# Two of nine blocks turn x and q on TensorE instead of VectorE, and block 0 makes its sums of h in two parts

## The chip, the core and the metric

The kernel runs on one core of a Trainium2 chip. The metric is the device time of one execution in microseconds (us); the median of three runs of the kernel before is 1025.14 us. In the profile TensorE is PE, VectorE is DVE, ScalarE is ACT, GpSimd is POOL, and SP is the engine that only issues DMAs. PEld is the loading of weights into TensorE, which overlaps with PE.

## What is computed

An attention without softmax for 8 batches and 8 heads (576 tokens, head size 64), a norm, and a gated feed-forward network, all in float32:

```python
kv = np.einsum('bhsd,bhse->bhde', k, v)
out = np.einsum('bhsd,bhde->bhse', q, kv)
rms = np.sqrt(np.mean(out * out, axis=-1, keepdims=True) + 1e-06)
out = out / rms * g_norm
x = out.transpose(0, 2, 1, 3).reshape(4608, 512)
g = x @ w_gate                       # 512 x 1536
silu = g * (1.0 / (1.0 + np.exp(-g)))
return (silu * (x @ w_val)) @ w_out  # 1536 x 512
```

## The kernel before

The 4608 tokens are cut into nine blocks of 512 (`BLK`); block n takes the last rows of batch n-1 and the first of batch n. Each block has two parts.

**Attention (class `Att`).** `load_kv` and `load_q` bring k, v and q into tiles of the pool `ld` (four buffers). `kv` makes the 64 x 64 products of k and v (L314) into the PSUM pool m (two buffers). `turn` transposes q, so that `product` (L355) can multiply it with kv; `product` also squares the result on ACT and sums it on DVE. `root` takes 1/sqrt by eleven small DVE instructions, `scale` multiplies, and the result has to be transposed again into `x`, with the gain applied on ACT; `sums` makes the sums of parts of x that the feed-forward part needs.

There are two ways to transpose. On PE: a product with the identity into PSUM (`turn_q`, L335, for q; `turn_x`, L402, for x), then a copy by ACT or DVE. On DVE: the stream transpose turns squares of 32 x 32 (L329 for q, L412 for x), and DMAs put these squares in place: on loading, for q (`load_quarters`, 32 small DMAs a block), and for x by `place_x` (L426, 16 DMAs, half on SP's queue, half on ACT's). `TURNED` is the first block whose x goes the second way; `quarters` says the same for q. In the kernel before, block 0 goes the first way and blocks 1 to 8 the second.

**Feed-forward (class `Ffn`).** The products are made by a scheme with seven products in place of eight (Strassen, Winograd's form), as in class `Quad`: products are numbered 1 to 7, and their order is written out by hand. Block 0 makes its up products plainly (`plain_up`, L1018), while the weights arrive and are rounded; `plain_end` then makes the sums of h, and `Down` multiplies h with `w_out` (L551). Block 1 uses the scheme once (`Up`, L551). Blocks 2 to 8 (`DEEP` is 2) use it twice, nested (`Inner`, L714); the summed weights that they need, the leaves, are made by DVE during block 1 (`leaf_steps`) and sent to DRAM (w), and each later block streams them from there through the tiles t (`Stream`, L795: nine buffers, 51 chunks of up to 256 KB a block). The last leaves, those of the weight pairs 4 and 5, stand in the list `latest` and are made during block 1's down stage. Down products 5, 7 and 4 use differences of `w_out` in nine t tiles, made by POOL (`turn_t`); `Stream.enable` opens the stream of the next block.

During the down stage of block n, the attention of block n+1 is laid between the down products: `steps` gives a table from the number of a product to what follows it. Where x goes the second way the whole of the product follows down product 1, `place_x` down product 5, and gain and sums down product 2:

```python
return {1: whole, 5: self.place_x, 2: end}          # n >= TURNED
return {1: lambda: self.half(0, ...), 6: middle, 2: last}   # otherwise
```

Otherwise the product is made in two halves, with `turn_x(0)` and the second half behind down product 6 and `turn_x(1)` behind down product 2; the order of the down products is then 1, 5, 6, 7, 2, 4, 3 in place of 1, 6, 5, 7, 2, 4, 3. In one f32 product of PE the profile counts two pieces, so a down product is 24 pieces of 256 columns.

The order of instructions on an engine is not that of the text alone. A scheduler simulates the engines and issues what is ready, by priority in the order of the text; `tc.issue_after` and `tc.keep_in_program_order` tie an instruction behind another on its engine.

Of the kernel before, what the change touches and what calls it, by code (L numbers as in the profile page):

```python
# [14 lines left out]
P = 128  # L15
# [3 lines left out]
def kernel(  # L19
# [173 lines left out]
    class Att:  # L193


        def __init__(self, n):
            self.n = n

            self.cut, half = divmod(n, 2)
            self.split = half * D  # L200
            self.ps, self.z = {}, None
            self.q, self.k, self.v, self.room = [], {}, {}, None
            self.halves = []
            self.quarters = n > 0

        def parts(self, t):

# [58 lines left out]
                    )  # L266
                    views[j] = t.rearrange("p h (t d) -> p h t d", t=KT)

        def load_quarters(self, i, pairs=(0, 1)):


            if pairs[0] == 0:
                self.q.append(ld_pool.tile([P, LD], F32, name="ld")[:, 0 : 2 * BLK])
            to = self.q[i].rearrange("p (j g d) -> p j g d", j=2, d=P // 4)
            cut = 2 * self.n
            spans = [(self.n - 1, S - D * self.n, 0, cut), (self.n, 0, cut, BLK // 32)]
            for j in pairs:
                for r in range(4):
                    h, d = divmod(r, 2)
                    for b, s0, g0, g1 in spans:  # L280
                        if g1 > g0:
                            nc.sync.dma_start(  # L282
                                out=to[32 * r : 32 * (r + 1), j, g0:g1],
                                in_=q[b, 4 * i + 2 * j + h, s0 : s0 + 32 * (g1 - g0), 32 * d : 32 * (d + 1)].rearrange(
                                    "(g p) d -> p g d", p=32
                                ),
                            )

        def load_q(self, i):
            if self.quarters:  # L290
# [127 lines left out]
        def place_x(self):  # L418
            src = self.turned.rearrange("p i (x c) -> p (i x) c", c=P)
            self.x = x_pool.tile([P, 7, 2, HB], F32, name="x")  # L420
            dst = self.x[:, 0:4].rearrange("p o k (t c) -> p (o k t) c", c=P)
            rows = [slice(32 * r, 32 * (r + 1)) for r in range(4)]
            for a in range(4):
                for b in range(4):
                    queue = nc.scalar if b % 2 else nc.sync
                    placed = queue.dma_start(out=dst[rows[b], :, rows[a]], in_=src[rows[a], :, rows[b]])  # L426
                    if b % 2 == 0:
                        self.placed = placed

        def gain_x(self):  # L430
            for i in range(2):
# [93 lines left out]

    DEEP = 2

    TURNED = 1

    class Quad:  # L530

# [41 lines left out]
    class Up(Quad):  # L573
# [51 lines left out]
        def multiply(self, p):  # L625
            super().multiply(p)
            ffn = self.ffn
            if ffn.n != DEEP - 1:
                return

            if p == 5:
                self.leaf_room = ring().rearrange("p f (s c) -> p (f s) c", c=P)
            if p in (5, 7, 4):
                at = 3 * (5, 7, 4).index(p)
                ffn.making.extend(leaf_steps(self.j, [(self.w[p].unsqueeze(1), (p,))], self.leaf_room[:, at:]))
            if p == 3:
                if ffn.leaf_room is None:
                    ffn.leaf_room = x_pool.tile([P, 3, 7, P], F32, name="xi").rearrange("p a b c -> p (a b) c")
                halves = lambda t: t[self.j].rearrange("p (o i) c -> p o i c", o=2)
                steps = lambda room: leaf_steps(self.j, [(halves(wg), (1, 2)), (halves(wv), (6, 3))], room)  # L640
                if self.j < NP - 2:
                    ffn.later.extend(steps(ffn.leaf_room))
                else:
                    ffn.latest.append(steps)

# [195 lines left out]
    class Down(Quad):  # L841
# [23 lines left out]
        def multiply(self, p):  # L865
            super().multiply(p)
            if p in self.t:
                stream.free((self.ffn.n, p))
            if p == 7:
                stream.enable(self.ffn.n + 1)  # L870
            stream.pump()

# [20 lines left out]
        def after2(self):  # L893
            add(nc.vector, self.o1[:, :, 0:HD], self.ps["a"], self.s)
            if self.final:
                self.ffn.store(self.o1[:, :, 0:HD], 0, slice(0, HD))

            pairs = self.ffn.h.rearrange("p (j e) t -> p e j t", e=2)
            self.s4 = sub(nc.vector, pairs[:, 1, :, 0:HB], pairs[:, 1, :, 0:HB], pairs[:, 0, :, HB:BLK])

        def after7(self):
            o = ring()
# [25 lines left out]
    class Ffn:  # L928
# [52 lines left out]
        def down(self, nxt):  # L981

            down = self.down_
            fill = nxt.steps() if nxt else {}
            for p in (1, 6, 5, 7, 2, 4, 3) if 5 in fill else (1, 5, 6, 7, 2, 4, 3):
                if p == 1:
                    down.turn_t(7, self.ended)
                if p == 6:
                    down.turn_t(4, nxt.halves[0] if nxt and nxt.n >= TURNED else None)

                with tc.issue_after(nxt.multiplied.ins) if self.n == 0 and p in (5, 6) else ExitStack():
                    down.multiply(p)
                self.make(12)
                if p in fill:
                    fill[p]()
                if p in (5, 7) and self.n == DEEP - 1:

                    with tc.issue_after(nxt.scaled.ins), tc.issue_after(nxt.placed.ins):
                        room = self.leaf_room if p == 5 else ring().rearrange("p f (s c) -> p (f s) c", c=P)
                        for step in self.latest.pop(0)(room):  # L1000
                            step()
                if p == 1:

                    with tc.issue_after(nxt.q_turned.ins) if self.n == 0 else ExitStack():
                        down.turn_s3()
# [20 lines left out]
        def plain_end(self):  # L1026

            self.s1 = s_pool.tile([P, NP, HB], F32, name="s1")
            self.h_sums(0, NP, nc.vector)
            self.down_ = Down(self)  # L1030
            self.down_.turn_t(5)

# [33 lines left out]
    for n in range(NB):  # L1066
        ffn = Ffn(n, blocks[n])
        nxt = blocks[n + 1] if n + 1 < NB else None
        if n == 0:

            with tc.issue_after(squared.ins), tc.issue_after(scaled.ins):
                weights(2)
            ffn.plain_up(0, (0,))
            copied = blocks[0].copied
            blocks[0].turn_x(1)
            for f in range(NF):
                with tc.issue_after(blocks[0].copied.ins if f else copied.ins):
                    weights(2 * (f + 2))
                ffn.plain_up(f) if f else ffn.plain_up(0, (1,))
            weights(len(pieces))  # L1080
            pairs = wo.rearrange("p (j e) d -> p e j d", e=2)
            t2(pairs[:, 0, :, HD:DM], pairs[:, 1, :, HD:DM], pairs[:, 0, :, 0:HD])
            nxt.room = x_pool.tile([P, 3, 7, P], F32, name="xi").rearrange("p a b c -> p (a b c)")

            with tc.issue_after(sent.ins):
                for i in range(2):
                    nxt.load_kv(i)
                for i in range(2):
                    nxt.load_q(i)
            ffn.plain_end()  # L1090
            for g in range(2):
                nxt.kv(g)
        else:

            def third():
                nxt.kv(0)
                nxt.load_kv(1)

            def two_thirds():
                nxt.kv(1)  # L1100
                if nxt.n == 2:
                    for i in range(2):
                        nxt.load_q(i)

            fill = {4: third, 8: two_thirds} if nxt else {}
            if n == DEEP:
                for a, at in enumerate((1, 2, 3, 5)):
                    fill[at] = lambda i=a // 2, j=a % 2: nxt.load_quarters(i, (j,))
            ffn.up(fill)
        if nxt:  # L1110
            nxt.turn()
        if 0 < n < NB - 2:
            blocks[n + 2].load_kv(0)
        if DEEP <= n < NB - 2:
            for i in range(2):
                blocks[n + 2].load_q(i)
        ffn.down(nxt)
        if n == 0:
            blocks[2].load_kv(0)

            with tc.issue_after(nxt.halves[0].ins):
                for j in range(NP // 2):
                    t2(wv[j][:, 0:2], wv[j][:, 2:4], wg[j][:, 0:2])
            with tc.issue_after(ffn.down_.s4.ins):
                for j in range(NP // 2, NP):
                    t2(wv[j][:, 0:2], wv[j][:, 2:4], wg[j][:, 0:2])


# [29 lines left out]
```

## Time and profile before

| | |
|---|---|
| three runs, median (lowest, highest) | 1025.14 us (1025.01, 1025.32) |
| the profiled execution | 1025.01 us, span 1023.2 us |
| PE busy, PEld busy | 1006.5 us, 896.9 us |
| DVE, ACT, POOL busy | 701.0 us, 228.0 us, 368.9 us |
| granted TensorE clock | 1.00 |
| first up product of block 0 | 29.7 us |
| block 0, down products | 116.3 to 155.8 us |
| block 1, up; down | 155.8 to 234 us; 234 to 272.9 us |
| DMA | 170.26 MB, mean 166 GB/s |

The profile is of one execution; its times are counted from the span's start. A group of instructions is given by its line in the kernel, engine, operation, and the tiles it writes and reads (`x<-r`). The chain is followed back from the last instruction, at each step to what released it. A busy time of PE comes from modelled ends, so the pace (how far apart starts are) says more than the busy share.

### The profile page before, as it was taken

How to read it: one execution, taken by the hardware profiler on the slowest of the kernel's cores; microseconds unless marked ns; L12 is line 12 of the kernel's file. 1: busy time of each engine (PE TensorE's matmuls, PEld its weight loads, DVE VectorE, ACT ScalarE, POOL GpSimd, SP SyncE). 2: the span in 40 equal slices, each digit the busy share in tenths (PEclk: the TensorE clock that was granted, in tenths of full speed). 3: DMA queues.
4: the chain of work that ended last, by engine and by line, in shares of the span. 5: the costliest groups of instructions: out<-in, count | busy, mean ns of one | idle time of the engine just before them, and what ended most of it. 6: DMA issues, size and time to landing. Idle time of an engine off the chain costs nothing.

```text
span 1023.2 us, 21404 instructions
## 1 busy us (share of the span) xinstructions
PE 1006.5 (98%) x8522; PEld 896.9 (88%) x8522; DVE 701.0 (69%) x1168; ACT 228.0 (22%) x352; POOL 368.9 (36%) x280
## 2 busy tenths in 40 slices
PE   6999999999999999999999999999999999999998
PEld 4544688888999989998999899988998999989997
DVE  2999688998666945685657566665669466946661
ACT  2766111221211212121121211111121211211110
POOL 0000263434045512561246315630555046513670
PEclk9999999999999999999999999999999999999999
DMA  8689633667888367855685568637772766066601
GB/s 224 201 264 275 127 70 113 184 150 167 246 219 245 70 164 204 253 100 119 209 243 146 89 199 246 183 57 200 231 197 50 175 196 188 20 165 205 189 29 42
DMA packets 273844, 170.26 MB, mean 166 GB/s; under 512 B 150608, under 2 KB 241872, under 8 KB 273744
## 3 DMA queue, kind: packets, MB, share of 16 engines
q1 hardware_dynamic: 238800, 164.42, 59.4%
q10 hardware_dynamic: 34880, 4.46, 2.7%
q8 instruction: 68, 1.11, 0.5%
q14 instruction: 32, 0.26, 0.1%
q0 software_dynamic: 64, 0.00, 0.0%
HBM read 138.02 MB, written 22.41 MB: 157 GB/s over the span
## 4 chain that ended last, share of the span: by engine, by line
PE 92%; DVE 3%; DMA 2%; SPq 1%; issue 1%; ACT 1%; DVEq 0%; ACTq 0%
PE b L714 26%; PE b L551 20%; PE c L714 13%; PE c L551 10%; PE a L714 6%; PE a L551 5%; PE b L1018 4%; PE c L1018 4%; PE m L314 2%; PE m L355 1%; DMA h<-in_v_dram 1%; SPq L282 1%; DVE xi L112 1%; DVE r L111 1%; DMA h<-in_k_dram 0%
## 5 line engine op out<-in xcount | busy, mean ns | idle before, releaser
L111 POOL TENSOR_TENSOR r<-r 128x256 f32<-128x256 f32 (+1 forms) x105 | 110.8, 1062 | 301.0 <-DVE r L111 241.1
L111 DVE TENSOR_TENSOR r<-b,r 128x512 f32<-128x512 f32 (+1 forms) x273 | 161.9, 606 | 65.6 <-PE b L714 60.6
L112 POOL TENSOR_TENSOR t<-wo 128x512 f32<-128x512 f32 x81 | 114.5, 1437 | 213.4 <-DVE wo L111 103.5
L111 DVE TENSOR_TENSOR r<-c,r 128x512 f32<-128x512 f32 (+1 forms) x179 | 108.4, 617 | 88.1 <-PE c L714 54.5
L714 PE MATMUL b<-x,t 128*128 128x128 f32 x1092 | 151.2, 275 | 0.0
L111 DVE TENSOR_TENSOR r<-a,r 128x512 f32<-128x512 f32 (+1 forms) x99 | 62.5, 631 | 113.5 <-PE a L551 71.1
L714 PEld LDWEIGHTS b<-x,t 128*128 128x128 f32 x1092 | 136.5, 192 | 0.8
L714 PE MATMUL c<-xi,t 128*128 128x128 f32 x840 | 112.4, 275 | 0.4 <-DVE xi L111 0.4
L113 POOL TENSOR_TENSOR h<-r 128x1024 f32<-128x1024 f32 (+1 forms) x40 | 81.9, 2064 | 78.1 <-DVE r L111 75.4
L714 PEld LDWEIGHTS c<-xi,t 128*128 128x128 f32 x840 | 102.9, 192 | 0.5 <-DVE xi L111 0.5
L551 PE MATMUL b<-wo,h 128*128 128x256 f32 x432 | 100.0, 383 | 0.1
L551 PE MATMUL b<-t,h 128*128 128x256 f32 x432 | 96.9, 381 | 0.0
L551 PEld LDWEIGHTS b<-t,h 128*128 128x128 f32 x432 | 81.5, 190 | 11.4 <-issue 0.2
L551 PEld LDWEIGHTS b<-wo,h 128*128 128x128 f32 x432 | 79.8, 190 | 13.0 <-DVE h L113 2.5
L728 ACT COPY r<-b 128x512 f32<-128x512 f32 x63 | 36.9, 586 | 211.5 <-PE b L714 206.4
L714 PE MATMUL b<-xi,t 128*128 128x128 f32 x588 | 79.7, 276 | 0.0
L714 PEld LDWEIGHTS b<-xi,t 128*128 128x128 f32 x588 | 72.4, 192 | 0.0
L714 PE MATMUL b<-x,wg 128*128 128x128 f32 x336 | 52.7, 279 | 0.2 <-DVE x L112 0.2
L714 PE MATMUL b<-x,wv 128*128 128x128 f32 x336 | 51.3, 275 | 0.0
L551 PE MATMUL a<-wo,h 128*128 128x256 f32 x216 | 48.3, 379 | 0.0
L551 PE MATMUL c<-wo,h 128*128 128x256 f32 x216 | 48.1, 379 | 0.0
L551 PE MATMUL c<-t,s 128*128 128x256 f32 x216 | 48.1, 379 | 0.0
(128 smaller groups left out, 1556.8 us busy)
## 6 DMA issues: line engine op xcount, KB each, us to landing
t<-w SPq DMA_DIRECT2D x336, 256.0 KB, 3.6
out_dram<-r SPq DMA_DIRECT2D x17, 512.0 KB, 3.1
ld<-in_k_dram SPq DMA_DIRECT2D x26, 288.0 KB, 5.3
ld<-in_v_dram SPq DMA_DIRECT2D x26, 288.0 KB, 6.3
ld<-in_moe_w_gate_dram SPq DMA_DIRECT2D x12, 512.0 KB, 4.9
ld<-in_moe_w_val_dram SPq DMA_DIRECT2D x12, 512.0 KB, 4.8
ld<-in_moe_w_out_dram SPq DMA_DIRECT2D x12, 512.0 KB, 5.0
w<-t SPq DMA_DIRECT2D x18, 256.0 KB, 3.3
```

What stands on the lines that cost most here:

```text
L111: add = lambda e, o, a, b: e.tensor_tensor(out=o, in0=a, in1=b, op=OP.add)
L112: sub = lambda e, o, a, b: e.tensor_tensor(out=o, in0=a, in1=b, op=OP.subtract)
L113: mul = lambda e, o, a, b: e.tensor_tensor(out=o, in0=a, in1=b, op=OP.mult)
L282: nc.sync.dma_start(out=to[32 * r : 32 * (r + 1), j, g0:g1], in_=q[b, 4 * i + 2 * j + h, s0 : s0 + 32 * (g1 - g0), 32 * d : 32 * (d + 1)]. ...
L314: nc.tensor.matmul(self.kv_ps[r][u * D : (u + 1) * D, g, :], lhsT=k[:, u, c, :], rhs=v[:, u, c, :], start=(c == 0), stop=(c == KT - 1),)
L355: self.multiplied = nc.tensor.matmul(self.ps[i][u][p : p + D, t, j, :], lhsT=self.qt[rows, 2 * i + t, j, p : p + D], rhs=kvs[b % 3][rows, ...
L551: nc.tensor.matmul(banks[e][:, e], lhsT=lhsT, rhs=rhs, start=first and i == 0 and (e == 0 or banks[0] is not banks[1]), stop=i == self.ste ...
L714: nc.tensor.matmul(ps[:, i, f], lhsT=self.weight(o, p, f), rhs=self.operand(o, p), start=first and (i, f) == (0, 0), stop=True, skip_group ...
L728: nc.scalar.copy(out=dst, in_=ps)
L1018: nc.tensor.matmul(t, lhsT=w[f // 2][:, i, P * (f % 2) : P * (f % 2 + 1)], rhs=x[:, i, of], start=(i == 0), stop=(i == NS - 1),)
```

## The change

The diff has these parts. `TURNED` goes from 1 to 3: x of blocks 1 and 2 is transposed by PE, and so is q of block 2, which is loaded whole; block 1's q stays on DVE (`n == 1 or n >= TURNED`), as do q and x of blocks 3 to 8. Block 3's q is asked for in block 1's down stage, behind its product 5, in place of four places in block 2's up stage. The leaves of pair 4 follow down product 1 of block 1 in place of 5, and those of pair 5 use `leaf_room` in place of a ring buffer; neither is tied to the placement of x any more. `Stream.enable` follows down product 4 in place of 7. The twelve `t2` sums of the up weights all follow the scaling of block 1's first half; before, the last six followed `s4`, a sum behind down product 2 of block 0. `plain_end` makes the sums of h for five pairs and then for the last pair, in place of all six at once.

```diff
-            self.quarters = n > 0
+            self.quarters = n == 1 or n >= TURNED
...
-        def load_quarters(self, i, pairs=(0, 1)):
-            if pairs[0] == 0:
-                self.q.append(ld_pool.tile([P, LD], F32, name="ld")[:, 0 : 2 * BLK])
+        def load_quarters(self, i):
+            ld = ld_pool.tile([P, LD], F32, name="ld")[:, 0 : 2 * BLK]
...
-    TURNED = 1
+    TURNED = 3
...
-                steps = lambda room: leaf_steps(self.j, [(halves(wg), (1, 2)), (halves(wv), (6, 3))], room)
+                steps = leaf_steps(self.j, [(halves(wg), (1, 2)), (halves(wv), (6, 3))], ffn.leaf_room)
...
-            if p == 7:
+            if p == 4:
                 stream.enable(self.ffn.n + 1)
...
+                if p == 5 and self.n == DEEP - 1:
+                    for i in range(2):
+                        self.loads(i)
...
-                if p in (5, 7) and self.n == DEEP - 1:
-                    with tc.issue_after(nxt.scaled.ins), tc.issue_after(nxt.placed.ins):
-                        room = self.leaf_room if p == 5 else ring().rearrange("p f (s c) -> p (f s) c", c=P)
-                        for step in self.latest.pop(0)(room):
+                if p in (1, 7) and self.latest:
+                    with tc.issue_after(nxt.scaled.ins):
+                        for step in self.latest.pop(0):
                             step()
...
-            self.h_sums(0, NP, nc.vector)
+            self.h_sums(0, NP - 1, nc.vector)
+            self.h_sums(NP - 1, 1, nc.vector)
...
-                if nxt.n == 2:
+                if nxt.n < TURNED:
                     for i in range(2):
                         nxt.load_q(i)
-            fill = {4: third, 8: two_thirds} if nxt else {}
-            if n == DEEP:
-                for a, at in enumerate((1, 2, 3, 5)):
-                    fill[at] = lambda i=a // 2, j=a % 2: nxt.load_quarters(i, (j,))
-            ffn.up(fill)
+            ffn.up({4: third, 8: two_thirds} if nxt else {})
...
-        if DEEP <= n < NB - 2:
-            for i in range(2):
-                blocks[n + 2].load_q(i)
+        if TURNED - 2 <= n < NB - 2:
+            ffn.loads = blocks[n + 2].load_q
+            if n >= DEEP:
+                for i in range(2):
+                    ffn.loads(i)
...
             with tc.issue_after(nxt.halves[0].ins):
-                for j in range(NP // 2):
-                    t2(wv[j][:, 0:2], wv[j][:, 2:4], wg[j][:, 0:2])
-            with tc.issue_after(ffn.down_.s4.ins):
-                for j in range(NP // 2, NP):
+                for j in range(NP):
                     t2(wv[j][:, 0:2], wv[j][:, 2:4], wg[j][:, 0:2])
```

More of the change, by code (lines that the diff above doesn't have):

```diff
@@ L267, in load_kv @@
                     views[j] = t.rearrange("p h (t d) -> p h t d", t=KT)
-        def load_quarters(self, i, pairs=(0, 1)):
-            if pairs[0] == 0:
-                self.q.append(ld_pool.tile([P, LD], F32, name="ld")[:, 0 : 2 * BLK])
-            to = self.q[i].rearrange("p (j g d) -> p j g d", j=2, d=P // 4)
+        def load_quarters(self, i):
+            ld = ld_pool.tile([P, LD], F32, name="ld")[:, 0 : 2 * BLK]
+            to = ld.rearrange("p (j g d) -> p j g d", j=2, d=P // 4)
             cut = 2 * self.n
             spans = [(self.n - 1, S - D * self.n, 0, cut), (self.n, 0, cut, BLK // 32)]
-            for j in pairs:
+            for j in range(2):
                 for r in range(4):
@@ L287, in load_quarters @@
                             )
+            self.q.append(ld)
         def load_q(self, i):
@@ L425, in place_x @@
                     queue = nc.scalar if b % 2 else nc.sync
-                    placed = queue.dma_start(out=dst[rows[b], :, rows[a]], in_=src[rows[a], :, rows[b]])
-                    if b % 2 == 0:
-                        self.placed = placed
+                    queue.dma_start(out=dst[rows[b], :, rows[a]], in_=src[rows[a], :, rows[b]])
         def gain_x(self):
@@ L639, in multiply @@
                 halves = lambda t: t[self.j].rearrange("p (o i) c -> p o i c", o=2)
-                steps = lambda room: leaf_steps(self.j, [(halves(wg), (1, 2)), (halves(wv), (6, 3))], room)
+                steps = leaf_steps(self.j, [(halves(wg), (1, 2)), (halves(wv), (6, 3))], ffn.leaf_room)
                 if self.j < NP - 2:
-                    ffn.later.extend(steps(ffn.leaf_room))
+                    ffn.later.extend(steps)
                 else:
@@ L898, in after2 @@
             pairs = self.ffn.h.rearrange("p (j e) t -> p e j t", e=2)
-            self.s4 = sub(nc.vector, pairs[:, 1, :, 0:HB], pairs[:, 1, :, 0:HB], pairs[:, 0, :, HB:BLK])
+            sub(nc.vector, pairs[:, 1, :, 0:HB], pairs[:, 1, :, 0:HB], pairs[:, 0, :, HB:BLK])
         def after7(self):
```

## The prediction

> **What bounds the kernel now.** I read the page first, then the waits of TensorE (PE), then the timelines around the block borders. The engines and the chain that ended last:
>
> ```profile
> PE 1006.5 (98%) x8522; PEld 896.9 (88%) x8522; DVE 701.0 (69%) x1168; ACT 228.0 (22%) x352; POOL 368.9 (36%) x280
> ...
> PE 92%; DVE 3%; DMA 2%; SPq 1%; issue 1%; ACT 1%; DVEq 0%; ACTq 0%
> ```
>
> TensorE holds 92% of the chain. Its waits show how little of the rest could be won:
>
> ```profile
> PE m L248 <- DMA h<-in_v_dram: 4.7, 2, 3.9
> PE b L335 <- DMA ld<-in_q_dram: 4.3, 1, 4.3
> PE c L551 <- DVE r L111: 1.6, 3, 0.7
> ```
>
> The first two lie in the first 14 us, where q, k and v arrive; the change leaves that part alone. After that only 1.6 us in three places is worth naming, all in block 1's up stage, where VectorE (DVE) is nearly full (71.26 us of 78.20 in the second line of the busy times by stretch; the first is block 4's down stage):
>
> ```profile
> 558.00:597.00 39.00, 38.98 (x331) 33.75 (x331) 24.20 (x37) 7.66 (x11) 9.05 (x6) 1.00 0.55 120
> 155.80:234.00 78.20, 76.58 (x451) 65.82 (x451) 71.26 (x133) 17.61 (x32) 31.47 (x23) 1.00 0.59 157
> ```
>
> After the stretch and its length the columns are PE, weight loads, DVE, ACT, POOL, granted clock, DMA share, GB/s. A busy PE need not be at its best pace, so I looked at the pace in the chain: 24 pieces of 256 columns take 5.18 us in every block, and one group of 64-wide products before them makes that 5.38:
>
> ```profile
> 144.73 0.72 PE m L314 x34
> 145.46 5.38 PE b L551 x24
> 150.83 5.18 PE c L551 x24
> ```
>
> The Trainium skill ("Trainium Kernel Development and Optimization", Best Practices) says to judge the distance from the peak by the weight loads, not by busy matmuls. That speaks against me: at 88% there would be 12% of room in which more matmuls might vanish. The constant pace speaks for the other reading, and I take the pace: **what is added to PE's queue lengthens the kernel by its own time.**
>
> **The change part by part.** *Transposes of blocks 1 and 2.* Before, VectorE turns q and x of blocks 1 to 8. After, `TURNED` is 3, and block 1 keeps its q on VectorE: x of blocks 1 and 2 and q of block 2 go to PE, 16 transposes each, 48 in all. Block 0 does its x this way already:
>
> ```profile
> 28.34 1.06 PE L402 MATMUL m<-ident,r 128*128 128x128 f32 x8 [0.28 <-DVE r L113]
> 29.74 1.99 PE L1018 MATMUL b<-x,wg 128*128 128x256 f32 x8 [0.34 <-ACT x L403]
> 31.57 0.93 PE L402 MATMUL m<-ident,r 128*128 128x128 f32 x7
> 32.59 1.99 PE L1018 MATMUL c<-x,wv 128*128 128x256 f32 x8
> ```
>
> One takes 0.27 us to its end, but they start (1.06 - 0.27) / 7 = 0.11 us apart. 48 x 0.11 = **5.3 us**, nothing beside it to hide in. The granted clock in 28 to 36 us is 1.00. The Trainium skill ("TensorE: Matmul & The Clock Gate", Part 4) gives about 275 ns for one transpose and says that they do not bring the full clock; one after another at that duration, 48 would be an estimated 13.2 us. The row has the same duration and a start distance of 0.11, so I stay with 5.3.
>
> *Borders on PE.* Leaving transposes for the long products costs: the seventh of the group at 31.57 starts at 32.23, the product at 32.59, so 0.36 - 0.11 = 0.25, and a first group of eight then takes 1.99 where others take 1.89: 0.35. Leaving a 64-wide group costs 5.38 - 5.18 = 0.20. Block 1 gets one more 64-wide group (its product now comes as two halves) and two groups of transposes, one of which runs into a 64-wide group (0.20 assumed): 0.20 + 0.35 + 0.20 = 0.75. Block 2 has the same and its q: 1.1. Together **1.9 us**, bounds 0.9 and 2.6.
>
> *PSUM.* `turn_x` fills both m tiles, and the half product behind it needs one back, after an ACT copy of 0.68 us (L403). The second four transposes cover 0.44 of that. The nearest rows are the idle times of 0.28 and 0.34 above: 0.3 for each of two blocks, **0.6 us**, bounds 0 (another product is placed between) and 1.4.
>
> *x of block 1 late.* Before, six of the twelve `t2` sums of the weights wait for `s4`; after, all twelve may run once block 1's first half is scaled (before: 131 us). Between 133.6 and 140.7 six of them took 7.1 us, slowed beside POOL's differences. Twelve take up to 14, and behind them on VectorE queue the sums, root and scale of block 1's second half, for which PE's second group of x transposes waits, four products (20 us) before the next up stage. I put the late ones at **0.6 us**, between 0 (the scheduler issues the half first) and 3.
>
> *VectorE.* Gone: six stream transposes (two for q, four for x) of 1.22 us each (L329, L412), 7.3 us. New: a second root per block, eleven small instructions from 126.35 to 128.78, 2 x 2.4, and a copy of 0.69: 5.5. Net 1.8 us lighter. One wait goes with certainty: block 2's q transpose on VectorE stood behind a DMA of r to w and ahead of the sums that free PE's c tile:
>
> ```profile
> 222.81 3.23 DMA w<-r
> ...
> 228.74 1.15 DVE r L329
> ...
> 232.31 1.99 PE c L551 x8
> ```
>
> PE idled 0.55 us there. **-0.5 us**, bounds -1.6 (all three idle times go) and 0.
>
> *Block 0's sums of h.* The two of 1.76 us each follow the last product of h (114.25); VectorE idled 6.18 us ahead of that. Five sixths, 2.9 us, move into that hole. What comes next is the transpose of block 1's q, then its product at 121.7 behind PE's first down product of 5.4 us, which starts with no wait. That down product is the cover; the q transposes ended at 120.8 and left 1 us of it. So **0**; without the cover, 2.9 us.
>
> *Placement of x, queues.* 32 DMA issues of x<-r go, 16 on SP, 16 on ACT, 0.64 and 0.69 us each; block 2's q comes with 4 issues, not 32. Neither queue was in the chain at these places. Block 3's q (32 issues of 0.46 us on SP) is now asked for at the third product of block 1's down stage. SP already issued half of it at 236 to 250, inside that stage and long before its place in the code: ready DMAs float forward. 0.
>
> *Leaves of weights.* Pair 4's go forward to behind the first product, pair 5's stay at p = 7, but write to `leaf_room`, which is block 2's `xi`. By before's row the last two sends from xi (384 KB) land 3.9 us after issue. Counted from the start of block 1's first down product, with 5.2 us a product and the added work: the second half's product ends at 19, its scale 7 us later at 26 (before: 240.7 to 248.3), eight leaf instructions (4.5 us from 250.6 before) at 30.5, the send at 35; the first sum into `xi` is due at 36, the up stage at 41. 0, and up to 4 us if this slips.
>
> *Weight stream.* `enable` moves from behind p = 7 to behind p = 4, in blocks 1 to 7. Before:
>
> ```profile
> 476.52 3.72 SPq L795 DMA_DIRECT2D t<-w  x6
> 484.64 0.38 SPq L938 DMA_DIRECT2D out_dram<-r  x1
> 485.12 1.87 SPq L795 DMA_DIRECT2D t<-w  x3
> ```
>
> ```profile
> 489.45 0.61 PE L714 MATMUL b<-x,t 128*128 128x128 f32 x4
> ```
>
> The first use of a chunk is at 489.45. If ready DMAs float forward as block 3's q did, the six are still issued near 476: 0, which I take, being the nearer row. If not, they queue behind the store of 484.64, start at 485.1, and land 3.6 us later at 488.7 at best, the next ones 0.7 to 1 us apart: 0.5 to 1 us late in each of seven blocks.
>
> **Sum.** 5.3 + 1.9 + 0.6 + 0.6 - 0.5 = 7.9 us on the profiled execution's 1025.01 (span 1023.2): 1032.9. The median of the three runs, 1025.14, lies 0.13 above it: **1033.0 us.** The bounds of these terms, not all taken at once, give 1029.5 to 1036.
>
> **The rivals.**
> *The stream comes late.* Against it the floating q loads, for it that `enable` stands behind the store in the code. 7 x (0.5 to 1) = 3.5 to 7 us more: 1036.5 to 1040.
> *Block 2's xi waits for pair 5's leaves.* For it the single buffer, against it the slack of about 5 us. Up to 4 us once: 1034 to 1037.
> *VectorE is the true bound of block 1's up stage, and the change makes the kernel faster.* It is 71.3 of 78.2 us busy there. The mechanism: lighter VectorE frees c tiles sooner. It decides only if what it frees exceeds PE's added 7.2 us; PE's idle time there is 1.6, so it would have to free 5.6 us that hide in PE's pace, which is the same there as elsewhere. Where it frees 1.6 us beyond what PE adds, the time is 1025.1 - 1.6 = 1023.5.
> *The transposes are not added as read* (the scheduler lays them into PE's waits): 5.3 - 1.6 = 3.7 and no more, 1028.8.
>
> **How the numbers follow.** Forecast 0.60; late stream 0.14; xi 0.13; transposes in the waits 0.08, of that 0.03 down to 1027; VectorE as the bound 0.05. The measurement can tell about 0.2%, 2.05 us, from no change. Faster by more than that comes from the VectorE rival: 0.04. Within it: the rest of that rival, 0.01, and those 0.03. Slower: 0.92. The range 1029.5 to 1038 leaves out the two low rivals and the upper half of the late stream, 0.20 together.
>
> **What would show it.** Right: 16 more L402 rows in each of block 1 and 2 and 16 of L335 behind block 1's up stage, about 0.11 us apart; x<-r down by 32; block 0's and block 1's down stages, 116.3 to 155.8 and 234 to 274.7 before, longer by about 3 and 5 us, the q turn counted; blocks 3 to 8 as long as before, 107.8 us from one to the next. Wrong: new PE waits on DMA t<-w at the head of blocks 2 to 8 (the stream), on DVE xi at the head of block 2 (the leaves), or PE's waits on DVE r in block 1 growing beyond 3 us; and any time below 1028.

## The result, and the profile after

| | before | after |
|---|---|---|
| median of four runs each | 1025.23 us | 1031.18 us |
| lowest to highest | 1025.01 to 1026.59 us | 1030.77 to 1032.34 us |
| ratio, 95% interval | | 1.0057, 1.004 to 1.0075 |
| the profiled execution, span | 1025.01, 1023.2 us | 1031.38, 1029.5 us |
| first up product of block 0 | 29.74 us | 30.61 us |
| block 0, down stage | 39.50 us | 41.37 us |
| head of block 1's up stage to block 2's | 116.89 us | 120.13 us |
| block 2 to 3 | 108.49 us | 108.31 us |
| blocks 3 to 4, 4 to 5, 5 to 6 | 107.78, 107.78, 107.73 us | the same |
| block 6 to 7, 7 to 8 | 108.43, 104.53 us | 108.78, 104.67 us |

The change makes the kernel 5.95 us slower by the medians; the forecast was 7.9. The spans differ by 6.3 us, but 0.87 of that lies ahead of block 0's first up product, in the load phase, which the change does not touch and which ended anywhere from 29.4 to 31.1 us in the fourteen profiles of this case. That leaves **5.42 us**, of which 1.87 + 3.24 = 5.11 lie in the two stages that the change rebuilds. Stages are taken from PE's first product in one to its first product in the next.

The page of after, the engines and the chain that ended last:

```profile
PE 1013.1 (98%) x8570; PEld 903.9 (88%) x8570; DVE 703.8 (68%) x1187; ACT 230.2 (22%) x359; POOL 370.4 (36%) x280
...
PE 93%; DVE 4%; DMA 2%; issue 1%; ACT 1%; SPq 0%; DVEq 0%; ACTq 0%
```

PE has 48 instructions more, the 48 transposes, and 6.6 us more of busy time. The three longest of PE's waits after the change (in total, how often, the longest; all in us but the count):

```profile
PE m L248 <- DMA h<-in_v_dram: 5.1, 2, 4.4
PE b L335 <- DMA ld<-in_q_dram: 4.3, 1, 4.3
PE c L549 <- DVE r L111: 1.1, 2, 0.7
```

So PE lost nothing to new waits; it has more to do. The busy times by stretch, block 1's up stage and block 4's down stage (columns as in the prediction):

```profile
161.40:230.00 68.60, 67.47 (x443) 58.38 (x442) 63.41 (x119) 15.32 (x28) 29.59 (x22) 1.00 0.67 184
...
564.00:603.00 39.00, 38.98 (x332) 33.75 (x331) 24.29 (x37) 7.66 (x11) 9.04 (x6) 1.00 0.55 120
```

DVE is still 92% full in the first line (63.41 of 68.60 us), at a granted clock of 1.00. Over a stretch as long as the 78.20 us of the prediction, from 158.56 us on, it is busy 69.49 us where it was 71.26. Block 4, which the change leaves alone, is the same to 0.1 us. What was added shows in the chain, in block 0's down stage (start, us, what; `...` stands for single 64-wide pieces):

```profile
134.57 0.87 PE m L402 x8
...
136.98 5.38 PE b L549 x24
142.36 5.18 PE a L549 x24
147.54 0.87 PE m L402 x8
148.41 5.18 PE b L549 x24
```

The first group of transposes runs into the second half of the 64-wide product, the second into a down product. That product keeps the pace of 5.18, so the border (the time that PE loses where it goes from one kind of group to another), for which I had assumed 0.35 behind transposes, is nothing here. Eight transposes take 0.87 in the chain, 0.11 each. The q of block 2, in PE's timeline:

```profile
232.15 0.60 PE L335 MATMUL m<-ident,ld 128*128 128x128 f32 x4
232.59 0.38 PE L335 MATMUL b<-ident,ld 128*128 128x128 f32 x2
...
236.83 0.60 PE L335 MATMUL m<-ident,ld 128*128 128x128 f32 x4
237.27 0.60 PE L335 MATMUL b<-ident,ld 128*128 128x128 f32 x4
```

Four transposes are 0.44 apart from the next four here too (236.83 to 237.27, 237.27 to the down product at 237.70), and one border shows: from the two at 232.59 to the next product, at 233.08, it is 0.49, which is 0.27 more than their own time. The products behind the two groups of q took 1.80 and 5.28 from start to start, for 1.73 and 5.18 elsewhere, so they lost another 0.1 each at most. The whole of PE's account, in us from the start of a group to the start of the next:

| | us |
|---|---|
| transposes: x of block 1 0.97 + 0.87, q of block 2 2.03, x of block 2 0.97 + 0.87 | +5.71 |
| product in halves: block 1 1.33 + 1.54 for 2.02 (+0.85), block 2 1.09 + 1.54 for 2.03 (+0.60) | +1.45 |
| third wait on DVE r in block 1 gone (1.6 to 1.1) | -0.5 |
| product of k and v no longer cut: block 0 -0.92, block 1 -0.44, block 2 -0.18 | -1.54 |
| sum | 5.12 |
| seen less load phase | 5.42 |

The fourth line was in no step of the forecast. The prediction's own chain shows one half of the product of k and v of block 2, the 34 pieces at 144.73, laid between two down products of block 0; the other 38 came in block 1's up stage. In after, PE's timeline has all 72 pieces in one place:

```profile
179.43 1.28 PE L314 MATMUL m<-ld 64*64 64x64 f32 x72
```

Two halves cost 0.72 + 0.74 and two borders of about 0.2, where one whole costs 1.21 and one border. Which stage gains depends on where the halves stood: block 0's down stage loses a half and a border (0.72 + 0.2), and block 2's up stage has 34 pieces more (+0.2) but two borders less (-0.4). The cut goes with the layout of the down stage. In the profiles with `TURNED` 2 the first product of block 2 alone is whole, with 3 those of blocks 2 and 3, with 6 those of blocks 2 to 6, and the later ones are cut as before. So the group stays whole where the down stage turns the next block's x on PE. Whether the transposes do it, or the other order of the down products that comes with them, no run separates.

The sums of h, on DVE's timeline of after (the first line is the new sum of five pairs):

```profile
106.41 1.48 DVE L111 TENSOR_TENSOR s<-h 128x1280 f32<-128x1280 f32 x1
...
115.87 1.42 DVE L111 TENSOR_TENSOR s<-h 128x256 f32<-128x256 f32 x1
117.32 1.37 DVE L112 TENSOR_TENSOR h<-s,h 128x256 f32<-128x256 f32 x1
118.61 1.23 DVE L329 STREAM_TRANSPOSE r<-ld 128x1024 f32<-128x1024 f32 x1
```

The five sixths did move ahead, but the last sixth takes nearly as long as they do. From the last product of h to the q transpose it is 2.8 us, where it was 3.5: of the 2.9 us expected, 0.7 was saved. Both small sums lie beside six sums of POOL (113.28 to 121.05, t<-wo). Even the 0.7 came to nothing, because the second q transpose then waited for the load of q:

```profile
121.27 1.25 DVE L329 STREAM_TRANSPOSE r<-ld 128x1024 f32<-128x1024 f32 x1 [1.43 <-DMA ld<-in_q_dram]
```

It ended at 122.52, 0.1 us ahead of the product that needs it (122.62).

### The profile page after: what moved, and what is told of

It reads as the page before. It is cut to its first block, busy times and chain, and to the rows that moved or that the text cites. A ratio compares the mean times of both kernels' runs of the same rounds, so it can differ in the third digit from the quotient of the medians.

```text
span 1029.5 us, 21442 instructions
## 1 busy us (share of the span) xinstructions
PE 1013.1 (98%) x8570; PEld 903.9 (88%) x8570; DVE 703.8 (68%) x1187; ACT 230.2 (22%) x359; POOL 370.4 (36%) x280
## 4 chain that ended last, share of the span: by engine, by line
PE 93%; DVE 4%; DMA 2%; issue 1%; ACT 1%; SPq 0%; DVEq 0%; ACTq 0%
PE b L712 26%; PE b L549 21%; PE c L712 13%; PE c L549 10%; PE a L712 6%; PE a L549 5%; PE b L1018 4%; PE c L1018 4%; PE m L314 1%; PE m L355 1%; DVE xi L112 1%; DMA h<-in_v_dram 1%; DVE r L112 1%; DVE r L111 1%; PE c L480 1%
```

## The experiments

Each ratio is against runs of the kernel before on the same chip. "Theory" is the forecast's: what is added to PE's queue counts, and the rest of the change costs nothing.

**The transposes without three of the other parts.** The new places of the leaves and the early request of block 3's q stay. After, with the sums of h at once, `enable` behind product 7 and the last six `t2` sums behind `s4`:

```diff
-            if p == 4:
+            if p == 7:
...
-            self.h_sums(0, NP - 1, nc.vector)
-            self.h_sums(NP - 1, 1, nc.vector)
+            self.h_sums(0, NP, nc.vector)
...
-                for j in range(NP):
+                for j in range(NP // 2):
...
+            with tc.issue_after(ffn.down_.s4.ins):
+                for j in range(NP // 2, NP):
...
```

> The kernel after with three of its edits undone: sums of h made at once, the stream opened behind down product 7, the last six t2 sums behind s4. Left of the change are the transposes on TensorE, the leaves and block 3's q. Theory (TensorE's queue: what is added to it lengthens the kernel, the rest is hidden): as slow as the kernel after, 1031 us, +5.5 to +6.5 against before. Rival (the edits undone here have a share in the loss): 1 us or more below the kernel after.

Measured: 1030.68 against 1025.04, 1.0055 (1.0042 to 1.0068). The whole loss stays. Block 0's down stage is 42.10 here, 0.7 longer than after's 41.37: the first half of the product took 1.89 where after's took 1.33, because it had to wait for the transposes of q on DVE. Both of them stood behind the sums of h, which took 2.87 and 2.71 us here beside POOL (1.76 each in before) and ended at 120.26; all of q had landed by 119.93. In this kernel the split might therefore have saved the 0.5. That is no rule: a later kernel with the split (`TURNED` 6, below) has 42.20, because there the second transpose waited for the load of q, which landed at 122.54 (in after at 121.15). The leaves and block 3's q were not tried alone. The parts of block 1 in the account above add up to 3.5, against 3.24 seen, so no loss is left for them to explain.

**One block alone.** The kernel before, with block 1's x turned on PE:

```diff
-    TURNED = 1
+    TURNED = 2
```

> The kernel before with TURNED = 2: only block 1's x goes to TensorE, 16 transposes, its product in two halves; q and x of block 2 stay on VectorE. Theory: block 0's down stage grows as in the kernel after, from 39.5 to 41.4 us, and the time by +1.9 us (1.3 to 2.5). Rival (the loss stands in one place, block 2's q or leaves): +0.5 or less here. Rival (late x, because the second half is scaled later): a wait of TensorE for x at the head of block 1, +3 or more.

Measured: 1027.28 against 1025.04, 1.0021 (1.0012 to 1.003); block 0's down stage 41.54, expected 41.4. The loss sits where the transposes are. The next stage, block 1 to 2, is 1.0 shorter in this profile (115.88), with one wait on DVE r of 0.7 left of the 1.6; more on that wait below.

**The sums of h alone.** The kernel before, with the split:

```diff
-            self.h_sums(0, NP, nc.vector)
+            self.h_sums(0, NP - 1, nc.vector)
+            self.h_sums(NP - 1, 1, nc.vector)
```

> The kernel before with the sums of h in two parts, nothing else. Theory: 0 (within 0.7 us), because TensorE did not wait for them. VectorE reaches the transpose of block 1's q by less than the 2.9 us counted, since the small sums behind the last product of h run beside GpSimd. Rival (the split is a gain that the transposes hide in the kernel after): faster by 1 us or more.

Measured: 1025.78 against 1025.04, 1.0004 (0.9995 to 1.0013); block 0's down stage 39.51 as before. The split, one of the two things that the title names, is worth nothing measurable.

**Is there a cover?** The kernel before, with the first of the two sums of h made three times:

```diff
             add(engine, s1, a21, a22)
+            if k == NP:
+                for _ in range(2):
+                    add(engine, s1, a21, a22)
```

> The kernel before, but VectorE makes block 0's first sum of h three times, 2 x 1.76 = 3.5 us more ahead of the transposes of block 1's q. The prediction named down product 1 as the cover of these sums, with about 1 us left. Theory: block 1's product on TensorE comes 2.5 us later than down product 1's end, TensorE waits or takes another product first: +0 to +2.5 us, with the wait on VectorE visible near 122 us if the order of TensorE is kept. Rival (the cover is much larger than read): no wait and no change in time.

Measured: 1027.52 against 1025.47, 1.0021 (1.0011 to 1.0031). PE's waits have a new first place outside the load phase:

```profile
PE m L355 <- DVE r L329: 2.0, 2, 1.7
```

Two sums more, 3.7 us on DVE, cost 2.1 (block 0's down stage is 2.3 longer): the down product hid some 1.4 of them, where the forecast read 1 us as left over. It also says why the split brings nothing: it shortens a chain that already had 1 us to spare. In the profile of the split alone the second q transpose waited 2.17 us for the load of q, so that the load, and no longer the sums, set when the transposes ended.

**The stream alone.** The kernel before, with `enable` behind product 4:

```diff
-            if p == 7:
+            if p == 4:
```

> The kernel before with the stream opened behind down product 4 in place of 7, nothing else. Theory (ready loads float forward): from block 3 on the six loads of chunks still stand ahead of the store of the output, time within 0.5 us of before; in block 1, where the stream opens for the first time, some loads may come later without a wait of TensorE. Rival (late stream): waits of TensorE for chunks at the heads of blocks, +3.5 to +7 us.

Measured: 1025.43, 1.0006 (0.9997 to 1.0015). SP's queue in this kernel:

```profile
475.82 3.06 SPq L795 DMA_DIRECT2D t<-w  x6
484.23 0.38 SPq L938 DMA_DIRECT2D out_dram<-r  x1
```

The six chunks still go ahead of the store, although the code asks for them behind it. In after it is the same:

```profile
481.47 3.58 SPq L793 DMA_DIRECT2D t<-w  x6
490.46 0.38 SPq L936 DMA_DIRECT2D out_dram<-r  x1
```

The rival of the late stream falls.

**Three blocks more.** After, with blocks 3 to 5 turned on PE as well; block 3's q is then loaded whole, so its early request in block 1 is left out:

```diff
-    TURNED = 3
+    TURNED = 6
...
-                if p == 5 and self.n == DEEP - 1:
+                if p == 5 and self.n == DEEP - 1 and TURNED == 3:
```

> The kernel after with TURNED = 6: q and x of blocks 3, 4 and 5 go to TensorE as well, 96 transposes more; block 3's q is loaded at two thirds of block 2's up stage. Theory (TensorE's queue, no cover): each further block costs what block 2 cost, 32 x 0.11 = 3.5 us for the transposes and about 0.6 for the broken product, less one border where the product of k and v is no longer cut: 3.5 to 4.3 us a block, +10.5 to +13 us over the kernel after, 1042 to 1044 us. Rival (VectorE is relieved, and deep blocks gain from it): under +6 us.

Measured: 1043.82 against 1025.47, 1.0175 (1.0158 to 1.0192): 18.35 over before, 12.4 more than after, 4.1 for each block added. By stages, blocks 2 to 3, 3 to 4 and 4 to 5 take 111.55 each, where after has 108.31, 107.78 and 107.78. That is 3.2, 3.8 and 3.8, or 10.8 in all; of the rest 0.8 lies in block 0's down stage (the late q above) and 0.6 in block 5 to 6. These blocks have a DVE with time to spare (busy 24 of 39 us in the stretch above) and lose about the same as block 2.

**Only q back on DVE.** After, with block 2's q loaded in quarters and turned on DVE:

```diff
-            self.quarters = n == 1 or n >= TURNED
+            self.quarters = n > 0
```

> The kernel after with block 2's q turned by VectorE as before (quarters for every block from 1 on); x of blocks 1 and 2 stays on TensorE. Theory: 16 transposes and their borders, 2.0 us by the trace of the kernel after, go, and TensorE's idle time of about 0.5 us ahead of c<-x,wv near 232 us, which stood in the kernel before behind the stream transpose, comes back: 1.5 us faster than the kernel after (1.0 to 2.0), about +4.4 against before. Rival (that idle time has nothing to do with q): 2.0 us or more faster than the kernel after.

Measured: 1029.04 against 1025.47, 1.0032 (1.002 to 1.0044). Block 1 to 2 takes 117.74, 2.39 less than after; the theory's 1.0 to 2.0 is missed, and the rival's 2.0 or more came. It counted on the third wait on DVE r to return with the q on DVE:

```profile
PE a L712 <- DMA t<-w: 1.0, 1, 1.0
PE c L549 <- DVE r L111: 0.7, 1, 0.7
```

It did not: one wait of 0.7 is left, where after has two with 1.1. The 2.03 of transposes and 0.4 of waits make the 2.4. (The first line is a wait in block 6 that neither before nor after has; it gives 1.0 us of the gain back.) So moving q is not what took the wait away, and the -0.5 of the forecast was booked on the wrong cause. Does the wait belong to the kernel before at all?

**The kernel before once more,** without an edit, for its profile.

> The kernel before, unchanged, for a second profile of it. In the first, block 1 took 116.9 us from the head of its up stage to that of block 2, with TensorE idle 1.6 us for VectorE in three places; in four kernels that are the same in this stage but for small edits elsewhere it took 115.9 to 116.1. Theory (the third of these waits, 0.5 us behind a late DMA of leaves, belongs to that one execution): 115.9 to 116.2 here. Rival (it belongs to the kernel): 116.7 to 117.

Measured: 1025.03. Block 1 to 2 takes 116.84 (116.89 the first time), and the wait is there:

```profile
PE c L551 <- DVE r L111: 1.5, 3, 0.7
```

It belongs to the kernel before, but hangs on little: in all eight other kernels here that turn block 2's q on DVE, these waits come to 0.7 to 1.0. The kernel with only `enable` moved has the same order of instructions up to there, and two waits with 0.9. Leaves are sent behind the 32 issues of q loads on SP; one of these issues took 2.04 and 2.00 us in the two executions of before, 1.21 in that kernel, and 0.43 with only the sums split. What makes an issue slow there stays open.

**The product of k and v whole.** The kernel before, with it tied behind the up unit that it stood in:

```diff
             def third():
-                nxt.kv(0)
+                with tc.issue_after(ffn.product_.ins):
+                    nxt.kv(0)
```

(`product_` is the last matmul of the unit before it.)

> The kernel before with the first product of k and v of each next block tied behind the up unit where it stands in the text, so that the scheduler can't lay half of it between down products 2 and 4. In the kernel before the two halves take 0.72 and 0.74 us and each brings a border of 0.1 to 0.25 into the products behind it; whole, such a product takes 1.2 us. Theory (borders on TensorE cost, and nothing waits where the half stood): 0.4 to 0.5 us less in each of five blocks that change, -2 us (-1 to -3). Rival (the half filled a wait of TensorE in front of down product 4): no change.

Measured: **1023.17 against 1025.47, 0.9979 (0.9971 to 0.9987)**, the lowest ratio of all, and better than both kernels. Block 0's down stage is 0.91 shorter, block 1 to 2 1.44 (of which 0.9 is waits on DVE r, which are down to 0.7), blocks 2 to 3, 3 to 4 and 4 to 5 0.45 each, block 5 to 6 0.24. Its chain in block 0's down stage, where before had 34 pieces of L314 and a 5.38:

```profile
139.93 5.18 PE a L551 x24
145.11 5.18 PE b L551 x24
150.29 5.18 PE c L551 x24
```

-0.91 is after's -0.92 in that stage, and 0.45 its 0.44 in block 1: the unforeseen gain of after is this one. So this experiment shows what the cut costs. Not all of the gain arrives; block 6 to 7 is 1.2 us longer, with a wait that was 0.4 before:

```profile
PE c L714 <- DVE xi L111: 1.0, 1, 1.0
```

**Two attempts on that wait.** Both keep the product whole. The first queues ACT's copy of down product 4 behind the gain of x, for which the sums into `xi` wait; the second queues DVE's sum of down product 3 behind these sums:

```diff
-            nc.scalar.copy(out=self.o2[:, :, 0:HD], in_=self.ps["b"])
+            with tc.issue_after(self.nxt.gained.ins) if self.nxt else ExitStack():
+                nc.scalar.copy(out=self.o2[:, :, 0:HD], in_=self.ps["b"])
```

> The kernel with the product of k and v kept whole, and one more edit: on ScalarE the copy of down product 4 is queued behind the gain of the next block's x. There that copy stood ahead of the gain at the head of block 6, the gain ran at 696.5, and TensorE waited 1.0 us for the sums into xi. Theory: that wait goes and the rest stays: 1.0 us less than with the product whole alone, about -3.2 us against before (-2.5 to -3.7). Rival (the copy then comes late and TensorE waits for the PSUM tile it frees): no gain or a loss against the product whole alone.

Measured: 1023.02 against 1024.69, 0.9984 (0.9975 to 0.9993). The gain ran early, at 693.97, but the wait of 1.0 stayed: on DVE the sum of product 3 still stood between the sums of x, at 703.10. The theory that the gain is late fails.

```diff
-            self.add_c(self.o1[:, :, HD:DM], self.u2)
+            with tc.issue_after(self.nxt.xi_made.ins) if self.nxt and self.nxt.n >= DEEP else ExitStack():
+                self.add_c(self.o1[:, :, HD:DM], self.u2)
```

> The kernel with the product of k and v kept whole, and on VectorE the sum of down product 3 queued behind the sums into the next block's xi. There, at the head of block 6, that sum stood in the middle of the sums of x and waited 1.2 us for TensorE to end product 3; moving the copy on ScalarE had not changed this. Theory (VectorE's order makes the wait): TensorE's 1.0 us for xi goes, the rest stays, about 1 us less than with the product whole alone, -3 us against before (-2.3 to -3.7). Rival (TensorE's own order at this place, which takes products of a ahead of those that need xi, was laid for the late sums and loses it again): no gain against the product whole alone, -2.2 us.

Measured: 1023.03 against 1024.75, 0.9985 (0.9976 to 0.9994). The wait only moved, from `xi` to `x`:

```profile
PE b L714 <- DVE x L112: 1.1, 1, 1.1
```

Neither brings more than the product kept whole does.

**The product of the attention at once.** After, with the 64-wide product of blocks 1 and 2 made whole behind down product 1, with one root, and only the transposes of x left at two places:

```diff
-            return {1: lambda: self.half(0, (m_psum, a_psum)), 6: middle, 2: last}
+            return {1: both, 6: lambda: self.turn_x(0), 2: last}
...
```

(`both` makes the two products, the root and the scaling, as `whole` does for the later blocks.)

> The kernel after, but the product of blocks 1 and 2 with kv is made at once behind down product 1, with one root, in place of two halves; the transposes stay on TensorE. By the trace of the kernel after the two halves take 2.87 and 2.63 us, by that of before the whole takes 2.02 and 2.03. Theory (a border and a wait for a PSUM tile, paid per group): 1.4 us faster than the kernel after (1.0 to 1.8), about +4.4 against before. Rival (the halves only show waits that move elsewhere): within 0.5 us of the kernel after.

Measured: 1029.97 against 1024.69, 1.0049 (1.0035 to 1.0062). The product takes 2.03 in both blocks, and the chain goes from the transposes straight into a down product:

```profile
135.04 0.87 PE m L402 x8
135.92 5.31 PE b L553 x24
```

Block 0's down stage is 0.90 and block 1 to 2 1.00 shorter than after's, 1.9 together, where the account above has 1.45 for the halves; 0.7 is given back in blocks 4 to 7. Less load phase the profile is 1.24 below after; the ratios, 1.0049 and 1.0057, do not separate the two kernels. That the halves cost PE about 1.5 us is seen in the rows; that the time follows is not shown by the medians.

## Why the prediction was right, and where it was off

Direction, mechanism and range held; the size was too large by 2.5 us of the 7.9 (5.42 seen).

- *Transposes, 5.3.* Right: 0.11 us from start to start, all 48 on the path. One block alone (+2.2 us) and three more (3.2 to 3.8 each in their own stages) agree. The two places of the Trainium skill that the prediction set against its rows are decided by these runs: with PEld at 88% there was no room in which matmuls vanished, as I had read out of the rule on weight loads ("Trainium Kernel Development and Optimization", Best Practices). And the transposes took 5.7, borders with them, not the 13.2 that I had estimated from the 275 ns of one ("TensorE: Matmul & The Clock Gate", Part 4).
- *Borders 1.9 and PSUM 0.6: mis-sized.* With the transposes the forecast had 7.8 for what PE gets to do, and 7.16 came. Behind transposes I had put 0.35 at each place where a long product follows. At two of these three places, behind a group of x, the product kept its 5.18; only the q came near it, with 0.27 and a product of 1.80 for 1.73. One row of block 0 was too little to price all three. The halves cost 1.45, more than the 0.4 of borders and 0.6 of PSUM set for them; how the 1.45 is shared between the two no run shows.
- *x of block 1 late, 0.6: nothing.* The sums and root of the second half did queue behind all twelve `t2` sums (from 141.15, the product having ended at 136.9), but the scale was done at 147.1 and the transposes started at 147.38, behind a down product. Only some 0.3 us were left.
- *The wait on DVE r, -0.5: the size right by luck, the cause not the one named.* With the q back on DVE it did not come back, and eight kernels that leave this q on DVE have less of it than the kernel before. "With certainty" was more than one profile could carry.
- *Sums of h, 0:* right, the cover shown by tripling one of them. That 2.9 us would move off the chain was wrong; it was 0.7, and the load of q took that back.
- *VectorE, 1.8 lighter:* so it is in the stretch of block 1's up stage (71.26 to 69.49 us), but over the whole span it is 2.8 heavier (701.0 to 703.8). The stream transposes went as counted (7.3); the new small instructions, and sums that ran longer than before, took more. The time did not depend on it.
- *The product of k and v: the step that was missing.* It was in the chain that I showed, cut at 144.73, and I used the row only for the price of a border. That the change would undo this cut was not asked. It is -1.5 of the 2.5 us; without it the loss would have been about 7.
- *The rivals.* Late stream: falls, by SP's queue in two kernels. Block 2's `xi`: the first sum into it ran at 272.75 and they ended at 277.1, ahead of the up stage at 278.74; PE did not wait. VectorE as the bound: falls. In block 1's up stage, where DVE is 92% busy, giving q back to DVE made the stage 2.39 shorter, and blocks 3 to 5, with a DVE that has room, lost 3.2 to 3.8 in their stages, near what block 2's own parts come to (3.87 of transposes and 0.6 of halves, less the product of k and v). Transposes in PE's waits: falls with the 5.7.

Of the 7.9: -0.65 borders and PSUM, -0.6 x late, -1.5 product of k and v, and +0.3 that I can't assign (block 6 to 8 is 0.5 longer than it was, blocks 0 and 1 0.2 shorter than the account).

## What to carry to other kernels

Where one engine keeps an even pace through the whole chain, count what a change adds to its queue, start to start; an engine that is 92% busy beside it can be relieved without any gain. Then look for what the scheduler will lay elsewhere once orders and lengths change: a group cut in two by it costs a second border, and tying it in place was worth more (2.2 us) than anything the change meant to do. Before a wait is booked as won, see whether it is there in a second profile and in neighbours of the kernel.

## What the runs showed of the hardware

Transposes of 128x128 f32 take 272 ns each to their end, but go 0.11 us apart at a granted clock of 1.00, and the step from them to the product behind costs between nothing (the product keeps its 5.18) and 0.27 us. Behind a group of 64-wide products it costs up to 0.2 (5.38).

A sum of 128x256 on DVE took 1.42 and 1.37 us beside POOL's sums of 1.26 to 1.46 us each. In the kernel before, block 1 makes twelve sums of this shape on DVE: eleven, which began while POOL stood still, took 0.41 to 0.43, and one, begun at 232.69 inside a POOL instruction (232.47 to 233.74), took 1.33. The Trainium skill ("SBUF — State Buffer", SBUF: two separate sides) says that DVE with two SBUF inputs and GpSimd share a port pair as an exclusive lock, held for a whole instruction. That fits: each of these sums took 0.9 to 1.0 us more, less than one POOL instruction. That it is the port, and a lock on it, no run here shows.
